# A shared pool of PSUM pairs, a planner with a clock and SiLU as one function, in an RWKV-7 scan followed by a SwiGLU layer

## The chip, the cores and the metric

The kernel runs on one core of a Trainium2 chip. The metric is device time in microseconds of one execution; three executions of the kernel before took 1606.69 to 1614.95 us, median 1608.68 us. Five engines work side by side: PE (TensorE, matrix products, with weight loads PEld that can overlap them), DVE (VectorE), ACT (ScalarE), POOL (GpSimd) and SP (SyncE), which here issues every DMA. Each engine runs its own instructions in the order in which the program gives them, and waits on semaphores for the others.

## The reference

Two blocks in a row. First a recurrent attention over S = 768 steps for 4 x 8 heads of width D = 40; then a feed-forward layer over the 3072 tokens of width 320 (8 heads x 40).

```python
for t in range(S):
    y[:, :, t] = einsum('bhd,bhde->bhe', r_t, state)
    Sa = einsum('bhde,bhe->bhd', state, a_t)
    state = state * w_t[:, :, None, :] - einsum('bhd,bhe->bhde', Sa, b_t) + einsum('bhd,bhe->bhde', v_t, k_t)
x = y as (3072, 320)
xn = x / sqrt(mean(x * x) + 1e-6) * rms_g
g = xn @ w_gate;  val = xn @ w_val            # 320 x 1536 each
out = (g * sigmoid(g) * val) @ w_out          # 1536 x 320
```

The scan's inputs are float32, the feed-forward weights float64: the kernel narrows them to float32 by bit operations. All matrix products are in float32.

## The kernel before, in words

**The work.** The 768 steps are cut into 24 chunks of C = 32 steps, all 32 heads at once. Per chunk there are four routines, all of which only *register* their operations with a planner:

- `front(c)` (line 337) loads w, a, k, b, v (ten DMAs), turns two of the tiles on PE, and walks five levels (1, 2, 4, 8, 16). Each level makes a group of 64 small matmul instructions `gr` (line 222, profile name `psB<-A,K`), a masked copy into `LT` (`where`, line 195), scalings of K and A on DVE, ACT and POOL, and from the second level on a turned copy `KN` (a transpose of eight 128x128 blocks, `turned`, line 317, profile name `psB<-ident,K`, and an ACT copy). It ends with DMAs that bring the chunk's 32 x 32 matrices through DRAM (`sB`) into the layout `M`.
- `inverse(c)` (line 401) inverts these unit triangular matrices on DVE: 31 steps of a product into `tmp` and a subtraction into `Yi` (lines 411 and 412, recorded under the helper's line 183), then DMAs back through `sY` into `LT`. There is one `M` tile.
- `main(c)` (line 421) carries the state over the chunk: products X, U, `up` and the new state `ST`; then the outputs `y` by one product with the state and five by levels, the root mean square, and the scaled, turned rows `xg`. Most of its PE pieces are groups of 64 small matmuls (`psC<-...`), five are transposes.
- `feed(g)` (line 535) does the feed-forward layer for two chunks once both `xg` parts are there: 12 slices f of the hidden width. Each slice loads `wf` (480 KB) and runs a group H (`psH<-xg,wf`, 12 matmul instructions of 256 columns), and each a group O (`psO<-wf,hT`, 4 instructions of 320 columns) which is added up in `psO` over all 12. Two slices share one H tile: after both H groups ACT takes the sigmoid of the gate half (512 columns, line 207), DVE multiplies gate and sigmoid, DVE multiplies by the value half into `hT`, and the two O groups follow.

`narrow` (line 568) is called 24 times ahead of the loop. Each call loads a part of the weights, and works it into float32 with seven DVE operations of 480 columns (lines 188, 192, 183: `sg<-wf`, `hT<-wf`, twice `sg<-sg`, `sg<-wf,sg`, `hT<-wf,hT`, `hT<-hT,sg`) and one on ACT (`hT<-hT`), and stores it to DRAM (`sW`). It borrows the buffers `wf`, `sg` (2) and `hT` (2) of `feed`.

**PSUM.** PSUM holds four tiles of [128, 2, 512] float32 (a pair of banks each), one per role (line 308): B for everything in `front`, C for everything in `main`, H and O for `feed`. The next user of a role's pair waits until the last one has been read out.

**The order.** `Plan` (line 26) is a list scheduler that runs while the program is built. `Plan.add` (line 46) registers a *piece* (one instruction, or one PE group) with an engine, a due time, an estimated time and its tiles; it derives which earlier pieces it needs from overlapping regions. `Plan.issue` (line 70) lets a simulated time run per engine: an engine that is free takes, of the pieces whose needs are met by then, the one due first. The order in which the pieces were taken is the program's order. Due times are laid out by a period of T = 46 per chunk: `front(c)` from (c - 2) T, `inverse(c)` from (c - 1) T + 4, `main(c)` from c T, the 12 slices of `feed(g)` from 2 (g + 1) T over two periods, `narrow` number f from -46 + 8 f. A PE group is taken as 0.6 to 2.2 us whatever the engine's clock; a DMA holds SP for 0.06 us and lands 2.2 us plus its bytes later, whatever else is moving.

Before all of this the program clears the tiles that are only partly written later: `Turns` (line 263) with its flag set clears them whole, on DVE and POOL by turns.

Of the kernel before, what the change touches and what calls it, by code (L numbers as in the profile page):

```python
# [7 lines left out]
FP32 = mybir.dt.float32  # L8
# [13 lines left out]
T = 46.0  # L22
EPS = 1e-6


class Plan:
# [3 lines left out]
    LATENCY = 0.1  # L30

    def __init__(self):
        self.pieces = []
        self.needs = []
        self.seen = {}

    @staticmethod
    def box(ap):
        dims = list(ap.ap)
        if ap.tensor.space == DRAM:  # L40
# [5 lines left out]
    def add(self, engine, due, time, issue, outs, ins, more=0.0):  # L46
        me = len(self.pieces)
        needs = set()
        mine = {}
        for aps, write in ((ins, False), (outs, True)):  # L50
            for ap in aps:
                key = ap.tensor.name, write
                a = self.box(ap)
                if key in mine:
                    b = mine[key]
                    a = min(a[0], b[0]), max(a[1], b[1]), min(a[2], b[2]), max(a[3], b[3])
                mine[key] = a
# [9 lines left out]
        self.pieces.append((engine, due, time, more, issue))  # L67
        self.needs.append(needs)

    def issue(self):  # L70
        n = len(self.pieces)
        users = [[] for _ in range(n)]
        missing = [len(d) for d in self.needs]
        for i, d in enumerate(self.needs):
            for j in d:
                users[j].append(i)
        ready = [0.0] * n
        free, waiting, order = {}, {}, []
        for i in range(n):
            free.setdefault(self.pieces[i][0], 0.0)  # L80
            waiting.setdefault(self.pieces[i][0], [])
            if not missing[i]:
                waiting[self.pieces[i][0]].append(i)
        for _ in range(n):
            best = None
            for e, w in waiting.items():
                if w:
                    t = max(free[e], min(ready[i] for i in w))
                    if best is None or t < best[0]:
                        best = t, e  # L90
            t, e = best
            i = min((i for i in waiting[e] if ready[i] <= t), key=lambda i: (self.pieces[i][1], i))
            waiting[e].remove(i)
            _, _, time, more, _ = self.pieces[i]
            free[e] = t + time
            order.append((t, i))
            for j in users[i]:
                ready[j] = max(ready[j], t + time + more + self.LATENCY)
                missing[j] -= 1
                if not missing[j]:  # L100
                    waiting[self.pieces[j][0]].append(j)
        for _, i in sorted(order):
            self.pieces[i][4]()
        self.order = sorted(order)
# [3 lines left out]
def kernel(  # L108
# [65 lines left out]
    plan = Plan()  # L174
# [6 lines left out]

    def tt(due, o, a, b, op):
        plan.add("DVE", due, 0.145 + 0.00104 * size(o), lambda: nc.vector.tensor_tensor(o, a, b, op), [o], [a, b])  # L183

    def ts(due, o, a, s1, s2, op1, op2=None):
        ins = [a] + [x for x in (s1, s2) if isinstance(x, bass.AP)]
        args = (op1,) if op2 is None else (op1, op2)
        plan.add("DVE", due, 0.145 + 0.00104 * size(o), lambda: nc.vector.tensor_scalar(o, a, s1, s2, *args), [o], ins)

    def stt(due, o, a, s, b, op1, op2):  # L190
        plan.add("DVE", due, 0.145 + 0.00104 * size(o),
                 lambda: nc.vector.scalar_tensor_tensor(o, a, s, b, op1, op2), [o], [a, b])

    def where(due, o, m, a):
        plan.add("DVE", due, 0.16 + 0.00104 * size(o), lambda: nc.vector.copy_predicated(o, m, a), [o], [m, a, o])  # L195

    def copy(due, o, a):
        plan.add("ACT", due, 0.16 + 0.00083 * size(o), lambda: nc.scalar.copy(o, a), [o], [a])  # L198

    def scale(due, o, a, by):  # L200
        ins = [a, by] if isinstance(by, bass.AP) else [a]
        plan.add("ACT", due, 0.16 + 0.00083 * size(o), lambda: nc.scalar.mul(o, a, by), [o], ins)  # L202

    def act(due, o, a, f, acc=None, **kw):
        if acc is not None:
            kw["accum_out"] = acc
        plan.add("ACT", due, 0.16 + 0.00083 * size(o), lambda: nc.scalar.activation(o, a, f, **kw),  # L207
                 [o] + ([acc] if acc is not None else []), [a])

    def ptt(due, o, a, b, op):  # L210
        plan.add("POOL", due, 0.2 + 0.0021 * size(o), lambda: nc.gpsimd.tensor_tensor(o, a, b, op), [o], [a, b])  # L211

    def pcopy(due, o, a):
        plan.add("POOL", due, 0.15 + 0.0014 * size(o), lambda: nc.gpsimd.tensor_copy(o, a), [o], [a])

    def dma(due, o, i, by="SP"):
        q, t = {"SP": (nc.sync, 0.06), "POOL": (nc.gpsimd, 1.0)}[by]
        n = size(i) * list(i.ap)[0][1]
        plan.add(by, due, t, lambda: q.dma_start(out=o, in_=i), [o], [i], 2.2 + n * 4 / 200e3)  # L219

    def mm(o, lhsT, rhs, start=True, stop=True):
        return o, lhsT, rhs, lambda: nc.tensor.matmul(o, lhsT, rhs, start=start, stop=stop, skip_group_check=True)  # L222

    def flip(o, i, ident):
        return o, i, ident, lambda: nc.tensor.transpose(o, i, ident)  # L225

    def pe(due, time, steps):
# [411 lines left out]
```

## Time and profile before

| | before |
|---|---|
| time, median of 3 (lowest, highest) | 1608.68 us (1606.69, 1614.95) |
| the profiled execution: time, span | 1605.55 us, 1603.8 us |
| PE busy, share of the span | 1384.5 us, 86% |
| DVE, ACT, POOL busy | 854.5, 441.6, 206.1 us |
| mean granted clock of PE | 0.902 |
| first and last H group start | 238.0, 1592.1 us |

How to read it: the page's first part has the busy time per engine; the second cuts the span in 40 slices of 40.1 us with the busy tenths of each engine and the granted PE clock. PE has two clock levels, 1.2 and 2.4 GHz; a granted clock of 0.50 is the lower one. The view of windows gives the busy time, the number of instructions (x) and the granted clock of any stretch. The timeline lists instructions in order of time, like ones merged, with the idle time before them and what ended it in brackets. The view of groups gives, per kind of instruction, the total busy time, the mean of one in ns, and the idle time of the engine just before them. Every helper records its own line, so groups are told apart by their tiles.

### The profile page before, as it was taken

What the parts mean: (1) busy time and instruction counts of PE and PEld (TensorE: products, weight loads), DVE (VectorE), ACT (ScalarE), POOL (GpSimd) and SP (SyncE); (2) the same over time, 40 slices, a digit from 0 to 9 for tenths busy, and PEclk for the clock granted to TensorE, in tenths of its full rate; (3) what the DMA queues carried; (4) which work ended last, traced back from release to release, by engine and by line L of the source; (5) the groups of instructions that cost most, each with busy time, mean ns of one, the idle gap of its engine ahead of it and who ended that gap; (6) DMA issues with size and microseconds to landing.
All of it is one profiled execution on the core that took longest, in us unless ns stands there. A gap on an engine that the chain in (4) does not pass through costs nothing.

```text
span 1603.8 us, 65497 instructions
## 1 busy us (share of the span) xinstructions
PE 1384.5 (86%) x29632; PEld 1110.6 (69%) x29632; DVE 854.5 (53%) x2767; ACT 441.6 (28%) x805; POOL 206.1 (13%) x360
## 2 busy tenths in 40 slices
PE   4556679889989999889989989989989989989766
PEld 3556677677777777667777777767778777767644
DVE  7777764545555565545555555644645554643211
ACT  2232323133323223232332323323323323212100
POOL 4110210111111110111110110110110110100000
PEclk9999979798999799798999789989989779799878
DMA  7453523243343343343343343333343344232211
GB/s 151 140 153 100 147 46 88 75 99 80 88 103 80 84 104 83 80 104 75 88 104 79 89 99 86 82 99 79 89 100 85 83 99 95 60 87 83 84 50 45
DMA packets 300246, 146.19 MB, mean 91 GB/s; under 512 B 263104, under 2 KB 276928, under 8 KB 299968
## 3 DMA queue, kind: packets, MB, share of 16 engines
q1 hardware_dynamic: 299968, 142.01, 36.4%
q8 instruction: 232, 3.80, 1.0%
q14 instruction: 46, 0.38, 0.1%
HBM read 125.83 MB, written 16.12 MB: 89 GB/s over the span
## 4 chain that ended last, share of the span: by engine, by line
PE 71%; DVE 8%; issue 6%; DMA 6%; ACT 5%; SPq 3%; POOL 1%; DVEq 0%; POOLq 0%; ACTq 0%
PE psH L222 22%; PE psC L222 17%; PE psO L222 11%; PE psB L225 9%; PE psB L222 7%; PE psC L225 5%; SPq L219 3%; DMA kbn<-in_b_dram 2%; DMA M<-sB 2%; ACT Xs L202 1%; DVE hT L183 1%; DVE y L183 1%; DMA sB<-LT 1%; ACT K L198 1%; DVE tmp L183 1%
## 5 line engine op out<-in xcount | busy, mean ns | idle before, releaser
L222 PE MATMUL psH<-xg,wf 128*128 128x256 f32 (+1 forms) x1728 | 411.8, 430 | 2.0 <-DVE xg L183 1.4
L222 PEld LDWEIGHTS psH<-xg,wf 128*128 128x128 f32 (+1 forms) x1728 | 278.3, 205 | 95.8 <-issue 55.4
L183 DVE TENSOR_TENSOR tmp<-Yi,M 128x60 f32<-128x60 f32 (+24 forms) x744 | 179.5, 241 | 98.8 <-DMA M<-sB 83.7
L222 PE MATMUL psO<-wf,hT 128*128 128x320 f32 x576 | 209.2, 490 | 19.1 <-DVE hT L183 18.3
L222 PEld LDWEIGHTS psB<-A,K 40*64 40x64 f32 x7680 | 154.9, 163 | 62.0 <-issue 30.0
L222 PE MATMUL psB<-A,K 40*64 40x16 f32 x7680 | 165.7, 226 | 32.2 <-ACT K L198 18.4
L183 DVE TENSOR_TENSOR Yi<-Yi,tmp 128x60 f32<-128x60 f32 (+24 forms) x744 | 177.3, 238 | 15.6
L225 PE MATMUL psB<-ident,K 128*128 128x128 f32 x960 | 152.7, 310 | 29.0 <-DVE LT L195 23.9
L198 ACT COPY KN<-psB 128x640 f32<-128x640 f32 x120 | 83.1, 693 | 293.9 <-PE psB L225 274.6
L183 DVE TENSOR_TENSOR sg<-psH,sg 128x512 f32<-128x512 f32 x72 | 49.7, 690 | 207.3 <-ACT sg L207 207.3
L225 PEld LDWEIGHTS psB<-ident,K 128*128 128x128 f32 x960 | 125.2, 160 | 39.7 <-DVE LT L195 24.9
L222 PEld LDWEIGHTS psO<-wf,hT 128*128 128x128 f32 x576 | 106.9, 206 | 55.1 <-DVE hT L183 21.8
L211 POOL TENSOR_TENSOR A<-A,T 128x256 f32<-128x256 f32 x96 | 73.0, 760 | 525.5 <-ACT T L198 176.9
L222 PEld LDWEIGHTS psC<-As,KN 64*64 64x64 f32 x6144 | 110.0, 147 | 37.2 <-issue 32.5
L222 PE MATMUL psC<-As,KN 64*64 64x16 f32 x6144 | 118.7, 216 | 17.8 <-issue 10.0
L183 DVE TENSOR_TENSOR K<-K,T 128x512 f32<-128x512 f32 (+1 forms) x192 | 100.5, 523 | 57.6 <-PE psB L225 38.2
L207 ACT ACTIVATE sg<-psH 128x512 f32<-128x512 f32 x72 | 43.1, 598 | 289.6 <-PE psH L222 289.5
L195 DVE COPY_PREDICATED LT<-msk,psB 128x256 f32<-128x256 uint32 x120 | 66.1, 551 | 88.4 <-PE psB L222 87.1
L198 ACT COPY K<-K 128x256 f32<-128x256 f32 x240 | 87.4, 415 | 32.8 <-DVE K L183 28.6
L183 DVE TENSOR_TENSOR y<-y,psC 128x256 f32<-128x256 f32 (+1 forms) x192 | 58.8, 318 | 67.9 <-PE psC L222 66.3
L183 DVE TENSOR_TENSOR As<-psC,msk 128x256 f32<-128x256 f32 x120 | 41.9, 414 | 45.9 <-PE psC L222 45.9
L225 PE MATMUL psB<-ident,kbn 128*128 128x128 f32 x192 | 37.1, 357 | 27.2 <-DMA kbn<-in_b_dram 21.3
(96 smaller groups left out, 1384.1 us busy)
## 6 DMA issues: line engine op xcount, KB each, us to landing
wf<-sW SPq DMA_DIRECT2D x144, 480.0 KB, 3.5
M<-sB SPq DMA_DIRECT2D x96, 128.0 KB, 3.5
sW<-hT SPq DMA_DIRECT2D x24, 240.0 KB, 3.4
wan<-in_w_dram SPq DMA_DIRECT2D x48, 80.0 KB, 3.1
wan<-in_a_dram SPq DMA_DIRECT2D x48, 80.0 KB, 3.1
kbn<-in_k_dram SPq DMA_DIRECT2D x48, 80.0 KB, 3.1
kbn<-in_b_dram SPq DMA_DIRECT2D x48, 80.0 KB, 3.2
VU<-in_v_dram SPq DMA_DIRECT2D x48, 80.0 KB, 2.7
```

The lines of the kernel that those rows point to most:

```text
L183: plan.add("DVE", due, 0.145 + 0.00104 * size(o), lambda: nc.vector.tensor_tensor(o, a, b, op), [o], [a, b])
L195: plan.add("DVE", due, 0.16 + 0.00104 * size(o), lambda: nc.vector.copy_predicated(o, m, a), [o], [m, a, o])
L198: plan.add("ACT", due, 0.16 + 0.00083 * size(o), lambda: nc.scalar.copy(o, a), [o], [a])
L202: plan.add("ACT", due, 0.16 + 0.00083 * size(o), lambda: nc.scalar.mul(o, a, by), [o], ins)
L207: plan.add("ACT", due, 0.16 + 0.00083 * size(o), lambda: nc.scalar.activation(o, a, f, **kw), [o] + ([acc] if acc is not None else []), [a])
L211: plan.add("POOL", due, 0.2 + 0.0021 * size(o), lambda: nc.gpsimd.tensor_tensor(o, a, b, op), [o], [a, b])
L219: plan.add(by, due, t, lambda: q.dma_start(out=o, in_=i), [o], [i], 2.2 + n * 4 / 200e3)
L222: return o, lhsT, rhs, lambda: nc.tensor.matmul(o, lhsT, rhs, start=start, stop=stop, skip_group_check=True)
L225: return o, i, ident, lambda: nc.tensor.transpose(o, i, ident)
```

## The change

- `Plan` is given three PSUM pairs and a list of eight stand-in tensors. A stage that needs PSUM takes `plan.room()`; which pair it gets is chosen in `issue` when its first piece is taken: a piece that opens a room is not ready until a pair is free, and the pair is free again when the room's last piece is done. H, B and C stages all draw on these three; O keeps a pair of its own.
- `issue` has a clock of its own for PE, at 1.0 or 0.5, that follows the `columns` of the pieces it has put into the last stretch, by the constants in the class; times of PE pieces are divided by it. Pieces with `columns` of 500 or more are H (2560), O (1280), the transposes of eight blocks (1024); all others count 0, but `xg`'s transposes (384). When the clock is low, or few columns have been streamed lately, PE takes only such pieces if any can go. Pieces marked `paced=True` (H and O) are held back until the due time of the pieces of `main` (`paced=None`) comes near.
- The estimates change: 0.08 us more per PE group, a DMA holds SP for 0.45 us and takes its turn in one lane of 180 GB/s.
- `feed` works slice by slice: H, then SiLU as one ACT function on 256 columns, one DVE product of 256 columns, and O due one slice later. Its due times are 10 later (`LAG`).
- `narrow` is due from 60 + 6 f. Of its DVE operations two become ACT functions (Relu with scale and bias) and the last a POOL product.
- Tiles of which only the padding must be zero are cleared there alone. In `main` the two groups of X, and the first groups of y, change places.

```diff
 class Plan:
-    LATENCY = 0.1
+    LATENCY = 0.15
+    WINDOW, ENOUGH, KEEP = 3.41, 1600, 1300
+    LOOK, LOW = 1.0, 1400
+    AHEAD, FAR = 4.0, 30.0
...
+    def room(self):
+        name = list(self.stand_ins)[len(self.rooms) % len(self.stand_ins)]
+        self.now[name] = len(self.rooms)
+        self.rooms.append([0, None, None])
+        return self.stand_ins[name]
...
+        def put(i):
+            p = P_[i]
+            (held if p.paced and p.due > pace + self.FAR else waiting[p.engine]).append(i)
+        def at_least(i):
+            p = P_[i]
+            return max(p.ready, min(pairs)) if p.room is not None and self.rooms[p.room][1] is None else p.ready
...
+            t, e = min((max(free[e], min(at_least(i) for i in w)), e) for e, w in waiting.items() if w)
+            can = [i for i in waiting[e] if at_least(i) <= t]
+            if e == "PE":
+                at = int(t / self.WINDOW)
+                while len(clock) <= at:
+                    c = columns.get(len(clock) - 1, 0)
+                    clock.append(1.0 if c >= (self.ENOUGH if clock[-1] < 1 else self.KEEP) else 0.5)
...
+                many = [i for i in can if P_[i].columns >= 500]
+                if many and (clock[at] < 1 or had < self.LOW):
+                    can = many
+                else:
+                    can = [i for i in can if not P_[i].paced or P_[i].due <= pace + self.AHEAD] or can
+            i = min(can, key=lambda i: (P_[i].due, i))
...
+                if room[1] is None:
+                    room[1] = min(range(len(pairs)), key=lambda q: pairs[q])
+                    pairs[room[1]] = float("inf")
+                room[0] -= 1
+                if not room[0]:
+                    pairs[room[1]] = end + self.LATENCY
...
-    plan = Plan()
+    plan = Plan([psum.tile([P, 2, 512], FP32, name=f"ps{i}") for i in range(3)],
+                [dram.tile([P, 2, 512], FP32, name=f"room{i}") for i in range(8)])
...
-    def dma(due, o, i, by="SP"):
-        q, t = {"SP": (nc.sync, 0.06), "POOL": (nc.gpsimd, 1.0)}[by]
-        plan.add(by, due, t, lambda: q.dma_start(out=o, in_=i), [o], [i], 2.2 + n * 4 / 200e3)
+    def dma(due, o, i):
+        plan.add("SP", due, 0.45, lambda at: nc.sync.dma_start(out=o, in_=i), [o], [i], lane=max(0.5, n * 4 / 180e3))
...
-                (nc.vector, nc.gpsimd)[i % 2].memset(t, 0.0)
+                (nc.vector, nc.gpsimd)[i % 2].memset(zero(t), 0.0)
...
-    ps_ = {t: Turns(n, [P, 2, 512], "ps" + t, pool=psum) for t, n in (("C", 1), ("B", 1), ("H", 1), ("O", 1))}
+    po_ = psum.tile([P, 2, 512], FP32, name="po")
...
-            act(d + 4, sg, h[:, 0], AF.Sigmoid)
-            tt(d + 4, sg, h[:, 0], sg, MUL)
-            tt(d + 5, hT, h[:, 1], sg, MUL)
+            act(d + 3, sg, h[:, 0], AF.Silu)
+            tt(d + 4, hT, h[:, 1], sg, MUL)
...
+        act(d, exf, ex, AF.Relu, scale=-1.0, bias=c1151)
+        act(d, ex, exf, AF.Relu, scale=-8388608.0, bias=c255)
-        ts(d, ex, ex, -896.0, 0.0, ALU.add, ALU.max)
-        ts(d, ex, ex, 255.0, 8388608.0, ALU.min, ALU.mult)
-        tt(d, m, m, ex.bitcast(FP32), MUL)
+        ptt(d, m, m, exf, MUL)
...
-        d = -T + 8 * f
+        d = N0 + NF * f
```

Here `N0, NF = 60.0, 6.0`, and `T = 46.0` as before.

## Rows read from the trace of the kernel before

**Rows 1.** The page: busy times, and the granted clock in 40 slices.

```profile
PE 1384.5 (86%) x29632; PEld 1110.6 (69%) x29632; DVE 854.5 (53%) x2767; ACT 441.6 (28%) x805; POOL 206.1 (13%) x360
...
PEclk9999979798999799798999789989989779799878
```

**Rows 2.** Windows: stretch, length, busy time (count) per engine, PEclk, DMA share, GB/s.

```profile
0.00:204.40 204.40, 121.27 (x2386) 107.91 (x2387) 153.15 (x443) 56.88 (x106) 42.05 (x73) 1.00 0.55 136
204.40:238.00 33.60, 25.25 (x791) 22.51 (x789) 18.67 (x76) 9.58 (x20) 4.77 (x8) 0.70 0.30 55
238.00:1472.00 1234.00, 1140.12 (x25115) 909.02 (x25112) 658.28 (x2196) 361.75 (x655) 157.70 (x275) 0.89 0.37 88
1472.00:1534.80 62.80, 48.43 (x1161) 38.07 (x1160) 16.08 (x42) 9.11 (x17) 1.57 (x4) 0.84 0.22 71
1534.80:1603.80 69.00, 49.40 (x192) 33.09 (x192) 8.30 (x12) 4.27 (x7) 0.00 (x0) 0.90 0.18 55
```

**Rows 3.** Timeline of PE, start and length in us: light groups, early and after 204 us.

```profile
21.73 1.91 PE L222 MATMUL psB<-A,K 40*64 40x16 f32 x64 [5.04 <-ACT K L198]
...
46.71 1.97 PE L225 MATMUL psB<-ident,K 128*128 128x128 f32 x8 [0.78 <-ACT KN L198]
...
205.65 1.12 PE L222 MATMUL psB<-A,K 40*64 40x16 f32 x64
```

**Rows 4.** Timeline of PE from 279 us: before and after a heavy group.

```profile
279.08 1.91 PE L222 MATMUL psC<-As,KN 64*64 64x16 f32 x64
...
286.95 3.90 PE L222 MATMUL psH<-xg,wf 128*128 128x256 f32 x12
...
296.23 2.63 PE L222 MATMUL psH<-xg,wf 128*128 128x256 f32 x12
```

**Rows 5.** Groups of PE between 238 and 1472 us: busy, mean ns, idle before.

```profile
L225 PE MATMUL psB<-ident,kbn 128*128 128x128 f32 x152 | 27.2, 338 | 21.6 <-DMA kbn<-in_b_dram 20.4 <-ACT A L198 0.6 <-DMA wan<-in_w_dram 0.3
...
L225 PE MATMUL psC<-ident,x 128*128 128x128 f32 x60 | 15.6, 371 | 17.6 <-ACT x L202 17.0 <-POOL x L214 0.7
```

**Rows 6.** Windows of the first two inversions, all operations.

```profile
53.80:90.40 36.60, 17.95 (x356) 15.74 (x354) 34.88 (x124) 9.30 (x19) 4.91 (x9) 1.00 0.46 135
109.70:173.50 63.80, 38.87 (x920) 35.31 (x920) 47.98 (x156) 17.09 (x32) 6.55 (x9) 1.00 0.45 124
```

**Rows 7.** The same windows, only what uses Yi.

```profile
53.80:90.40 36.60, 14.04 (x62) 0.00 (x0) 1.00 0.46 135
109.70:173.50 63.80, 15.30 (x62) 0.00 (x0) 1.00 0.45 124
```

**Rows 8.** The same windows, only what uses sg.

```profile
53.80:90.40 36.60, 16.00 (x32) 0.00 (x0) 1.00 0.46 135
109.70:173.50 63.80, 20.63 (x43) 0.00 (x0) 1.00 0.45 124
```

**Rows 9.** Groups by shape: what SiLU and narrow replace, and their nearest rows.

```profile
L183 DVE TENSOR_TENSOR sg<-psH,sg 128x512 f32<-128x512 f32 x72 | 49.7, 690 | 207.3 <-ACT sg L207 207.3
...
L183 DVE TENSOR_TENSOR As<-psC,msk 128x256 f32<-128x256 f32 x120 | 41.9, 414 | 45.9 <-PE psC L222 45.9
...
L207 ACT ACTIVATE sg<-psH 128x512 f32<-128x512 f32 x72 | 43.1, 598 | 289.6 <-PE psH L222 289.5
...
L198 ACT COPY y<-psC 128x256 f32<-128x256 f32 x24 | 8.9, 372 | 45.6 <-PE psC L222 45.6
...
L207 ACT ACTIVATE hT<-hT 128x480 f32<-128x480 int32 x24 | 14.5, 605 | 32.1 <-DVE hT L188 32.1
...
L211 POOL TENSOR_TENSOR Sdec<-ST,T 128x640 f32<-128x640 f32 x24 | 30.8, 1284 | 170.6 <-DVE ST L183 151.7 <-DVE Yi L183 18.8
...
L207 ACT ACT_TABLE_LOAD x1 | 1.3, 1283 | 0.0
```

**Rows 10.** Timeline of PE in the last feed, with its waits.

```profile
1544.14 1.34 PE L222 MATMUL psO<-wf,hT 128*128 128x320 f32 x4 [2.15 <-DVE hT L183]
...
1594.66 2.42 PE L222 MATMUL psO<-wf,hT 128*128 128x320 f32 x8 [2.15 <-DVE hT L183]
```

More of the change, by code (lines that the diff above doesn't have):

```diff
@@ L44, in box, with add @@
         return p, p + dims[0][1], f, f + sum(s * (n - 1) for s, n in dims[1:]) + 1
-    def add(self, engine, due, time, issue, outs, ins, more=0.0):
+    def add(self, engine, due, time, issue, outs, ins, **kw):
         me = len(self.pieces)
+        piece = Piece(engine, due, time, issue, **kw)
         needs = set()
@@ new lines, in add @@
+        piece.missing = len(needs)
+        for i in needs:
+            self.pieces[i].users.append(me)
+        if piece.room is not None:
+            room = self.rooms[piece.room]
+            room[2] = first = me if room[2] is None else room[2]
+            for i in needs:
+                if i < first and first not in self.pieces[i].users:
+                    self.pieces[i].users.append(first)
+                    self.pieces[first].missing += 1
+            room[0] += 1
+        self.pieces.append(piece)
@@ L224, in flip, with pe, issue @@
     def flip(o, i, ident):
-        return o, i, ident, lambda: nc.tensor.transpose(o, i, ident)
-    def pe(due, time, steps):
-        def issue():
+        return o, i, ident, lambda at: nc.tensor.transpose(at(o), i, ident)
+    def pe(due, time, steps, columns=0, paced=False, more=[]):
+        def issue(at):
             for s in steps:
-                s[3]()
-        plan.add("PE", due, time, issue, [s[0] for s in steps], [x for s in steps for x in s[1:3]])
+                s[3](at)
+        plan.add("PE", due, time + 0.08, issue, [s[0] for s in steps] + more, [x for s in steps for x in s[1:3]],
+                 columns=columns, paced=paced)
@@ L441, in main @@
                  U[rows(i, 1), :, 0:N * D].rearrange("p o (n d) -> p o n d", n=N))
-        up = ps_["C"].next()
-        pe(d + 8, 0.95, [mm(up[half(o), i, col(n)], kn(z, 32, i, n, o), VU[half(i), n, o, 0:D]) for n, i, o in each])
+        up = plan.room()
+        pe(d + 8, 0.95, [mm(up[half(o), i, col(n)], kn(z, 32, i, n, o), VU[half(i), n, o, 0:D]) for n, i, o in each], paced=None)
         if c + 1 < NCH:
@@ L479, in level @@
         def level(due, ps, j):
-            pe(due, 0.95, [mm(ps[half(o), i, n], kn(z, LEVELS[j], i, n, o), As[half(i), j, o * N + n]) for n, i, o in each])
+            pe(due, 0.95, [mm(ps[half(o), i, n], kn(z, LEVELS[j], i, n, o), As[half(i), j, o * N + n]) for n, i, o in each], paced=None)
         def down(due, j, ps):
@@ L514, in main @@
             down(d + 30 + q, j, yl[:, :, q])
-        xn = ps_["C"].next()
+        xn = plan.room()
         pe(d + 35, 0.6, [mm(xn[half(q), o, m * D:(m + 1) * D],
```

258 lines of the change are left out of this document (143 added, 115 removed).

## The prediction

> **What bounds the kernel now.** I read the page's busy times first: PE works 86% of the span, DVE 53%, so PE is the engine to account for, and the row of granted clocks shows that it is seldom at full speed for long [rows 1]. Then the windows by stage [rows 2]. Between 238 us, when the first H group starts, and 1472 us PE is busy 1140 of 1234 us at a granted clock of 0.89: 94 us idle, and, as the two levels are 1.0 and 0.5, (1 - 0.89) x 2 = 22% of the stretch, 271 us, at the lower one. If PE is as busy there as elsewhere (92%), 250 us of its work ran at half speed and about 125 us of them are lost. So the stretch holds about 1140 - 125 = 1015 us of work at full clock. Before 238 us stand 238 us in which PE is busy 147 us with the scan alone. The stretch to 204 us reads 1.00, but only because the record of the clock starts there: a group of 64 small matmuls takes 1.91 us at 21 us and 1.12 us at 205 us, and the transposes at 46 us, 1.97 us, are at the lower level too [rows 3]. After 1472 us come 132 us of draining. Between 276 and 290 us is a typical loss: light groups at 1.91 us, an H group that takes 3.90 us and pulls the clock up, and the next H at 2.63 us [rows 4].
>
> So the span is 1015 us of dense work, 125 us of half clock, 94 us of idle PE, 238 us of start and 132 us of end.
>
> **The change part by part**, on the profiled execution's own 1605.55 us (span 1603.8 us and 1.75 us around it; the median of the runs is 3.1 us above it).
>
> *A, the start: -45 us.* The state can't move to the next chunk before that chunk's inversion is done. The first takes 36.6 us and the second 63.8 us on DVE [rows 6], though their own 62 operations need only 14.0 and 15.3 us [rows 7]; operations on `sg`, all of them narrowing at this time, take 16.0 and 20.6 us of DVE in the same windows [rows 8]. `narrow` was due from -46, among the inversions; it is now due from 60, behind both, and three of its seven operations leave DVE. Counting only what is counted in rows 8, 16 + 20.6 = 37 us go. With one pair per role the front pass also waits at each step for a copy out of PSUM, 0.78 us in the row at 46 us [rows 3], and about ten such waits stand in the first pass: 8 us more. Bounds: 71 us, if both inversions fall to their own times, and 0, if the narrowing, which must end before the first H as it shares its buffers, now ends no earlier: its chain gets longer by one ACT step (605 ns in its row, twice, in place of two DVE steps) and a POOL step (under the 1284 ns of the 640-element product) [rows 9]. I take 45, nearest to what is counted. POOL and ACT have room, 13% and 28% busy [rows 1]. If that room failed, the queue behind a waiting `narrow` step on DVE is the inversion itself, and PE waits for that.
>
> *B, the clock from 238 to 1472 us: -80 us.* The new order puts H, O or transposes into any stretch that runs light. There are enough of them: a chunk has 6 H groups (2.63 us [rows 4]), 6 O groups (1.34 us [rows 10]) and about 10 transposes (about 1 us, half of the 1.97 us at the lower level [rows 3]): some 34 of the roughly 50 us that a chunk takes at full clock (1015 us for some 20 chunks in the stretch). Bounds: 0 and 125. The row at 286 us, where one H group brings the clock back, speaks for the far end; the order is fixed while the program is built, and PE's true times will slip against the planner's, so I leave about a third: -80.
> A row here differs from a rule. The clock first rises at 204 us, in a stretch of 64-matmul groups and transposes, 34 us before the first H: transposes at least don't prevent it [rows 2, 3]. The Trainium skill (TensorE: Matmul & The Clock Gate, Part 4, on PE-mode transpose) says that full rate does not engage for transposes, as they don't count as busy in the same way. By that rule only H and O would hold the clock, B would shrink towards 0 and the sum would be 1518 us in place of 1438 us; the first rival below has the same time from rows.
>
> *C, idle PE in the same stretch: -24 us.* Of the 94 us, 21.6 us stand before the transposes of `kbn`, waiting for its DMA, and 17.6 us before those of x, waiting for a chain over ACT and POOL [rows 5]. The new planner counts 0.45 us of SP per DMA in place of 0.06 and so will issue `kbn` earlier, and with three shared pairs PE has another stage's group to fill the second. Bounds: +94 (twice as much, from waits for pairs) and -94. I take the sum of the two rows, 39 us, less some 15 us for new waits. What is late next: PE itself.
>
> *D, the end: -22 us.* The last feed has PE to itself: in the 69 us from 1534.8 us it is busy 49.4 us [rows 2]. Two H groups fill the one H pair, then PE waits 2.15 us for sigmoid and two products, six times in all [rows 10]: 13 us, of which the last wait stays, shorter (one ACT function and one product). Of these 13 us I take 11. A granted clock of 0.90 means 20% of the window at the lower level, so some 10 us of the 49.4 us, of which 5 go with a PE that doesn't pause. From 1472 to 1534.8 us 14 us are idle; I take 6 of them, for feed slices held ready. Bounds 0 and 34 (all idle of both windows).
>
> *SiLU itself: 0.* DVE loses 72 products of 690 ns and turns 72 others of 512 columns into 144 of 256, 414 ns by the nearest row: about -39 us. ACT gets 144 functions, 372 ns by the copy of 256 columns from PSUM, for 72 of 598 ns: +11 us. Both lie beside PE; only in D is the chain on the path. If SiLU shared no activation table with the other functions, each of the 24 squares would cost two loads of 1283 ns [rows 9], 62 us of ACT, hidden by its idle time; I take 0, since sigmoid, copy and square need one load together in this trace after the first. If that cover went, the wait would stand before x.
>
> *Clearing padding only* shortens what DVE does ahead of the first chunk by a few us, inside A's bounds. The exchange of the two X groups, of y's groups and the later due times: 0; the instructions on PE stay the same.
>
> Sum: 45 + 80 + 24 + 22 = 171 us; 1605.6 - 171 = 1434.6, and 3.1 us for the median: **1438 us**.
>
> **The rivals.**
> *The heavy pieces don't hold the clock.* A, C and D come, B doesn't: 1438 + 80 = 1518 us. For it: the order of before had all these groups too and spent 22% at the lower level [rows 2]. Against it: one H group is followed by the full rate [rows 4].
> *Slower: the pool of three pairs starves PE.* A pair is now taken about 12 times per chunk by `front`, 11 by `main` and 3 by `feed`, 26 x 24 = 624 times. Each taker waits for a read-out that the planner has guessed, and PE's order is fixed: a late copy holds everything behind it, of all roles. If half of the takes meet the wait of 0.78 us [rows 3], that is 243 us: 1438 + 243 = 1681 us. It decides from (171 + 8) / 624 = 0.29 us per take on. Against it: a take holds a pair for about 3 us, 26 x 3 = 78 us per chunk of 50 us, on three pairs, which is half of what they offer.
> *The planner's clock is out of step.* The order comes out with the idle time and the half clock of before, and the longer narrowing chain eats A: 1605 us, nothing that can be told.
>
> **How the numbers follow.** The forecast case gets 0.70: its own range, from B and C at their better ends with A at 71 (1438 - 26 - 45 - 30 = about 1335), to A at 0 (1483 us). The clock rival gets 0.18 (1480 to 1560), out of step 0.04, starving 0.08. A measurement of this kernel tells about 0.5%, 8 us, from no change. Faster: 0.70 + 0.18 = 0.88; same 0.04; slower 0.08. The range from 1335 to 1545 us holds nearly all of the first case and four fifths of the second, a little over 0.8.
>
> **What would show it.** A: the first H before 200 us, both inversions under 45 us. B: a granted clock over 0.95 from the first H to 1470 us, and few H groups at 4 us or more. C: idle PE under 75 us in as long a stretch of work, without a large wait of PE on a copy or on DVE. D: under 58 us from the last `xg` to the end, H and O without gaps. SiLU: `sg` products gone, ACT at 144 functions near 372 ns, no table loads in the loop. Wrong it would be if PE waited for read-outs before many first groups of a pair (starving), or if the clock stayed near 0.89 while H, O and transposes are spread evenly (the clock rival).

## The result, and the profile after

The changed kernel takes **1429.48 us**, median of 4 runs (1421.51 to 1436.31); the kernel before takes 1607.68 us in the same comparison (4 runs, 1600.68 to 1614.95). The ratio is **0.889, with a 95% interval from 0.883 to 0.895**: 178 us faster. The profiled execution of after took 1430.57 us, span 1428.8 us; below it is set against the one of before with its span of 1603.8 us. In the comparison of E1 to E4 one execution of E1 and one of the kernel before were over 1.5% slower than the fastest of their kernel, and they are left out of the medians and ratios.

From the page of after: busy times, the granted clock in 40 slices of 35.7 us, and the engines' shares of the chain that ended last. They answer to [rows 1].

```profile
PE 1289.4 (90%) x29632; PEld 1048.9 (73%) x29632; DVE 851.9 (60%) x2695; ACT 486.5 (34%) x925; POOL 233.1 (16%) x386
...
PEclk8755666999997989999999989999999999999999
...
PE 51%; DVE 34%; issue 5%; SPq 4%; DMA 3%; ACT 3%; POOL 0%; DVEq 0%; POOLq 0%; ACTq 0%
```

PE runs the same 29632 instructions in 1289.4 in place of 1384.5 us. For equal instructions a shorter busy time means a higher clock, so some 95 us of the gain are clock. Idle PE (span less busy) falls from 219.3 to 139.4 us, 80 us. Together these are the whole 175 us of the two spans. The third row warns of what is next: a third of the chain stands on DVE now, where before it was 8%.

The windows of after by stage, in the columns of [rows 2]: to the first H; the dense stretch, to the end of the last front work; the drain, to the last `xg`; the last feed.

```profile
0.00:241.70 241.70, 171.59 (x4263) 156.83 (x4264) 192.98 (x538) 113.07 (x204) 83.25 (x119) 0.65 0.53 129
241.70:1315.00 1073.30, 1011.35 (x23768) 814.02 (x23768) 632.39 (x2081) 355.11 (x682) 148.28 (x264) 0.96 0.41 98
1315.00:1377.70 62.70, 62.63 (x1413) 48.25 (x1411) 20.88 (x66) 12.70 (x27) 1.57 (x4) 1.00 0.28 84
1377.70:1428.80 51.10, 43.87 (x192) 29.78 (x192) 5.62 (x13) 5.59 (x14) 0.00 (x0) 0.98 0.32 98
```

PE has two clock levels, and a stretch is taken to lose half of the busy time that it spends at the lower one (an estimate: a group of 64 takes 1.91 us there for 1.12). The table counts that record by record of the granted clock. Both traces read 1.00 up to their first record (204.4 us in before, 13.7 us in after), though the durations of PE's work show the lower level; this time is counted as low. By the rows' rounded clocks alone, (1 - clock) x busy, the dense stretch comes out alike: 125 and 40 us.

| stage | idle PE, before and after | lost to the clock | the rest: work at full clock |
|---|---|---|---|
| start, to the first H | 91.5, 70.1 | 67, 65 | 79, 107 |
| the dense stretch | 93.9, 62.0 | 120, 43 | 1020, 969 |
| drain and last feed | 34.0, 7.3 | 10, 0 | 88, 106 |
| sum | 219.4, 139.4 | 197, 108 | 1187, 1182 |

The work must come out equal in sum; its 5 us of difference show how exact the table is.

**Who PE waits for now.** Groups of PE in the dense stretch of after; columns as in [rows 5], whose two rows are the last two here.

```profile
L310 PE MATMUL ps<-ident,VU 128*128 128x128 f32 x160 | 23.2, 292 | 12.9 <-DVE tmp L270 8.7 <-DVE Yi L270 4.1
...
L310 PE MATMUL ps<-ident,ST 128*128 128x128 f32 x152 | 22.7, 297 | 26.3 <-DVE tmp L270 22.6 <-DVE Yi L270 2.1 <-DVE LT L270 1.6
...
L310 PE MATMUL ps<-ident,kbn 128*128 128x128 f32 x144 | 18.8, 273 | 0.0
...
L310 PE MATMUL ps<-ident,x 128*128 128x128 f32 x60 | 10.5, 284 | 0.0
```

The waits for `kbn`'s DMA (21.6 us) and for x (17.6 us) are gone, and new ones stand before the transposes of the state, of VU and of r. The profile puts them down to `tmp` and `Yi`, steps of the inversion. But no transpose of `main` reads either, so the name can't be taken as it stands. The largest of these waits, in the timeline of PE and then of DVE (start us, length us):

```profile
608.14 1.12 PE L307 MATMUL ps<-A,K 40*64 40x16 f32 x64
609.10 1.12 PE L307 MATMUL ps<-VU,KN 64*64 64x40 f32 x64
614.58 1.76 PE L310 MATMUL ps<-ident,VU 128*128 128x128 f32 x7 [4.36 <-DVE tmp L270]
```

```profile
613.33 0.23 DVE L270 TENSOR_TENSOR Yi<-Yi,tmp 128x72 f32<-128x72 f32 x1
613.48 0.42 DVE L270 TENSOR_TENSOR hT<-ps,sg 128x256 f32<-128x256 f32 x1
613.81 0.71 DVE L270 COPY_PREDICATED LT<-msk,ps 128x256 f32<-128x256 uint32 x1
614.32 0.25 DVE L270 TENSOR_TENSOR tmp<-Yi,M 128x68 f32<-128x68 f32 x1
```

`tmp` ends at 614.57 us, 0.01 us before PE starts, and so it is named. The masked copy `LT<-msk,ps` ends at 614.52, 0.06 us before: it reads the group `ps<-A,K` of 608.14 us out of its PSUM pair, and stood for over 4 us in DVE's queue, mostly behind inversion steps. Gone through one by one, the dense stretch has 33 waits of PE of over 0.3 us, 48 us in all, that end 0.054 to 0.056 us after such a copy, and 5 (8 us) that end as long after `hT<-ps,sg`. 4 of the 5 stand before another group of a shared pair, the fifth before an O. The program's own instructions name the buffer: in all 33 and in these 4 the waiting group writes the very pair that this operation has just read. So PE waits for a **pair to be read out**, and the read-out stands in DVE's queue among the inversion: from the end of the group that it reads to its own start, the 33 copies lose 95 us together, 79 us of them with inversion steps at work.

### The profile page after: what moved, and what is told of

Its sections match the earlier page's. It is cut to its first block, busy times and chain, and to the rows that moved or that the text cites. A ratio compares the mean times of both kernels' runs of the same rounds, so it can differ in the third digit from the quotient of the medians.

```text
span 1428.8 us, 65724 instructions
## 1 busy us (share of the span) xinstructions
PE 1289.4 (90%) x29632; PEld 1048.9 (73%) x29632; DVE 851.9 (60%) x2695; ACT 486.5 (34%) x925; POOL 233.1 (16%) x386
## 4 chain that ended last, share of the span: by engine, by line
PE 51%; DVE 34%; issue 5%; SPq 4%; DMA 3%; ACT 3%; POOL 0%; DVEq 0%; POOLq 0%; ACTq 0%
PE ps L307 35%; DVE Yi L270 11%; DVE tmp L270 11%; PE ps L310 8%; PE po L307 7%; SPq L304 3%; DVE K L270 3%; DVE T L270 3%; DVE LT L270 2%; DVE hT L270 1%; DMA sB<-LT 1%; DMA M<-sB 1%; DVE ST L270 1%; ACT sg L287 1%; DVE As L270 1%
## 5 line engine op out<-in xcount | busy, mean ns | idle before, releaser
L307 PE MATMUL ps<-xg,wf 128*128 128x256 f32 (+1 forms) x1728 | 389.2, 413 | 0.7 <-DVE xg L270 0.7
L307 PEld LDWEIGHTS ps<-xg,wf 128*128 128x128 f32 (+1 forms) x1728 | 262.1, 195 | 85.1 <-issue 52.2
L307 PE MATMUL po<-wf,hT 128*128 128x320 f32 x576 | 190.8, 458 | 0.4 <-DVE hT L270 0.4
L310 PE MATMUL ps<-ident,K 128*128 128x128 f32 x960 | 145.4, 307 | 26.3 <-DVE K L270 20.7
L307 PEld LDWEIGHTS ps<-A,K 40*64 40x64 f32 x7680 | 132.6, 142 | 40.9 <-issue 26.5
L307 PE MATMUL ps<-A,K 40*64 40x16 f32 x7680 | 143.5, 212 | 12.1 <-DVE hT L270 4.2
L310 PEld LDWEIGHTS ps<-ident,K 128*128 128x128 f32 x960 | 123.6, 158 | 37.0 <-issue 26.4
L307 PEld LDWEIGHTS po<-wf,hT 128*128 128x128 f32 x576 | 101.7, 195 | 31.8 <-issue 4.7
L307 PEld LDWEIGHTS ps<-As,KN 64*64 64x64 f32 x6144 | 108.1, 145 | 21.3 <-issue 13.4
L307 PE MATMUL ps<-As,KN 64*64 64x16 f32 x6144 | 116.3, 214 | 4.3 <-DVE As L270 3.0
```

What stands on the lines that cost most here:

```text
L307: return o, lhsT, rhs, lambda at: nc.tensor.matmul(at(o), lhsT, rhs, start=start, stop=stop, skip_group_check=True)
L310: return o, i, ident, lambda at: nc.tensor.transpose(at(o), i, ident)
```

## The experiments

All are edits of the changed kernel. Beside each span stand PE's busy time, and idle as span less busy, from the page of each run; the clock is that of the dense stretch, from the first H to the end of the last front work. The runs come from five comparisons, in which the kernel before had medians from 1600 to 1608 us; so differences between medians are good to some 8 us, and the ratios say more.

| run | median us | ratio to before, 95% | span | PE busy | idle | clock |
|---|---|---|---|---|---|---|
| after | 1429.48 | 0.889 (0.883 to 0.895) | 1428.8 | 1289.4 | 139 | 0.96 |
| E1 no clock | 1512.20 | 0.947 (0.933 to 0.960) | 1510.4 | 1358.7 | 152 | 0.92 |
| E2 roles | 1497.98 | 0.937 (0.930 to 0.945) | 1495.9 | 1317.6 | 178 | 0.95 |
| E3 sigmoid | 1459.11 | 0.913 (0.904 to 0.921) | 1463.4 | 1321.4 | 142 | 0.93 |
| E4 narrow at 0 | 1420.64 | 0.891 (0.883 to 0.900) | 1417.4 | 1281.0 | 136 | 0.95 |
| E5 same order | 1447.13 | 0.905 (0.900 to 0.910) | 1454.0 | 1301.1 | 153 | 0.95 |
| E6 old estimates | 1479.03 | 0.923 (0.918 to 0.928) | 1478.2 | 1300.8 | 177 | 0.94 |
| E7 lag 0 | 1416.62 | 0.884 (0.879 to 0.889) | 1416.5 | 1283.5 | 133 | 0.97 |
| E8 calibrated | 1441.01 | 0.901 (0.896 to 0.907) | 1434.5 | 1283.6 | 151 | 0.95 |
| E9 half inversion | 1297.18 | 0.810 (0.806 to 0.813) | 1293.7 | 1237.0 | 57 | 1.00 |
| E10 lag 0, narrow 0 | 1409.82 | 0.879 (0.876 to 0.882) | 1407.8 | 1269.8 | 138 | 0.97 |
| E11 lag 0, DVE +0.03 | **1363.42** | 0.852 (0.847 to 0.856) | 1361.9 | 1248.5 | 113 | 0.99 |
| E12 DVE model | 1420.51 | 0.887 (0.883 to 0.891) | 1416.3 | 1266.0 | 150 | 0.97 |

**E1: the planner's clock taken away.** It always counts full speed, and prefers nothing.

```diff
-        clock, columns, recent, lane, order = [0.5], {}, [], 0.0, []
+        clock, columns, recent, lane, order = [1.0], {}, [], 0.0, []
-                    clock.append(1.0 if c >= (self.ENOUGH if clock[-1] < 1 else self.KEEP) else 0.5)
+                    clock.append(1.0)
-                if many and (clock[at] < 1 or had < self.LOW):
+                if False:
```

> The changed kernel without the planner's clock: it takes PE to run at full rate always and no longer prefers H, O and transposes when few columns were streamed; the pool, the other estimates, SiLU and the narrowing stay. Theory 1 (the preference holds the clock): the dense stretch from the first H to 1315 us falls back from a granted clock of 0.96 to about 0.89, which gives back the 77 us of half clock: about 1505 us. Rival (the pool alone gives the order, the clock is a by-product): clock of 0.94 or more in that stretch, 1429 to 1445 us.

1512 us, 83 us more than after. The dense stretch of E1, in the columns of [rows 2]:

```profile
284.30:1382.60 1098.30, 1025.72 (x22714) 827.23 (x22713) 593.63 (x1975) 341.77 (x662) 146.06 (x254) 0.92 0.38 93
```

Of the 82 us between the spans PE's busy time takes 69, so it is the clock. In the dense stretch it falls only to 0.92, between the two forecasts: 88 us are lost there, counted as in the table above, against 43 in after and 120 in before. But the first H moves to 284 us, and 86 us are lost ahead of it, against 65 in after. Over the whole execution PE's busy time is 1384.5 us in before, 1358.7 us in E1 and 1289.4 us in after: 69 of the 95 us hang on the planner's clock and its preference for heavy groups, which E1 takes away together. What brings the other 26 us is not shown.

**E2: the pool taken away.** Three pairs as before, each bound to a role again; the rest of the planner stays.

```diff
-    def room(self):
+    def room(self, role):
-        self.rooms.append([0, None, None])
+        self.rooms.append([0, None, None, role])
-            return max(p.ready, min(pairs)) if ...
+            return max(p.ready, pairs[self.rooms[p.room][3]]) if ...
-                    room[1] = min(range(len(pairs)), key=lambda q: pairs[q])
+                    room[1] = room[3]
```

> The changed kernel with its clock, but the three pairs given one to each role again (front, main, feed), as before. Theory 1 (the preference holds the clock, the pool only saves idle time): granted clock still about 0.95 from the first H on, idle PE in that stretch up by the 32 us that the change took away: about 1460 us. Rival (the pool is what gives the planner a choice): clock back at 0.90 and idle up as well, 1530 us or more.

1498 us: the pool is worth some 69 us. The windows of drain and last feed of E2, in the columns of [rows 2], and PE's timeline at the start of the last feed:

```profile
1348.20:1434.90 86.70, 72.25 (x1408) 54.88 (x1406) 17.53 (x50) 12.85 (x26) 2.83 (x5) 0.83 0.24 71
1434.90:1495.90 61.00, 46.13 (x192) 30.92 (x192) 5.65 (x13) 5.29 (x13) 0.00 (x0) 0.95 0.21 62
```

```profile
1440.83 1.34 PE L307 MATMUL po<-wf,hT 128*128 128x320 f32 x4 [1.00 <-DVE hT L270]
1442.02 2.52 PE L307 MATMUL ps<-xg,wf 128*128 128x256 f32 x12
1445.48 2.63 PE L307 MATMUL ps<-xg,wf 128*128 128x256 f32 x12 [0.94 <-DVE hT L270]
```

The last feed has one pair again and waits 0.9 to 1.0 us at H and at O; the drain has idle time and half clock again. This is neither of the two times that had been expected. Idle time and loss of E2, counted stage by stage as in the table above, are over those of after by 14 us in the start, 20 us in the dense stretch (idle 71 us for 62, clock 0.95 for 0.96) and 36 us in drain and last feed. So the pool works most at the end.

**E3 and E5: SiLU as two steps again.** E3 takes a sigmoid and one more product of 256 columns on DVE, known to the planner. E5 keeps the order of after to the instruction: the product goes right ahead of the other, and the planner doesn't know of it.

```diff
-            act(d + 3, sg, h[:, 0], AF.Silu)
+            act(d + 3, sg, h[:, 0], AF.Sigmoid)
+            tt(d + 3, sg, h[:, 0], sg, MUL)
```

> The changed kernel with sigmoid on ACT and a product on DVE in place of SiLU, still slice by slice. Theory 1: 144 more products of some 0.42 us on DVE, 60 us, lie beside PE; no change, 1421 to 1437 us. Rival (the chain from H to O and DVE's queue are near the path, as the chain of waits is now 34% DVE): 1445 us or more, with PE waiting longer behind DVE.

> Sigmoid with an additional DVE product of 256 columns per slice, but the planner is told nothing of the product, so that every engine keeps exactly the order of the changed kernel. It parts two readings of the 30 us that sigmoid cost when the planner knew of it. Reading 1 (the longer chain and DVE's queue cost it): about 1455 to 1465 us again, the dense stretch at a granted clock near 0.93. Reading 2 (another order, that happens to hold the clock worse): 1425 to 1437 us, at 0.96.

E3 takes 1459 us, 30 more than after, as its rival had said; of the 35 us between the spans 32 are PE's busy time. E5 takes 1447 us, 18 more, which lies between its two readings. So about 18 us are the price of 144 more products in DVE's queue and the longer chain; the other 12, which are hardly clear of the noise, would come with another order. In the profiled execution of E5, its slowest, the waits that end 0.05 us after `LT` grow from 48 to 58 us and those after `hT` from 8 to 14: the product, in a queue that is idle for 37% of the span, makes read-outs late.

**E4 and E8: the narrowing earlier.** E4 lets it be due from 0 in place of 60. E8 does the same and also gives the planner H and transposes with the times that the trace of after shows.

```diff
-N0, NF = 60.0, 6.0
+N0, NF = 0.0, 6.0
```

> The changed kernel with the narrowing due from 0 in place of 60. Theory 1 (the first H, at 241.7 us, waits for the narrowing, whose last store is issued at 241.8 us, not for the scan, whose second xg is there at 193 us): first H at about 200 us, and the 40 us of earlier feed work fill light time: 1405 to 1415 us. Rival (earlier narrowing again pushes the inversions apart): second xg 20 us later or more, no gain, 1425 to 1445 us.

> Narrowing due from 0, and PE estimates moved to what the chip shows: 2.50 us for H (2.28 before), 0.95 us for eight transposes (1.03 before). If slip between the planner's clock and the chip's is what leaves 43 us of half clock in the dense stretch: half of that goes, about 1400 us. Rival (the slip comes from DVE and ACT, not from PE's own times): 1415 to 1430 us.

In E4 the last narrowed part is stored at 189 us and the first H starts at 194.6 us; in after they stand at 241.8 and 241.7 us. The rows of stores `sW` on SP's queue (first and last start), of E4 and then, for 225 to 250 us, of after:

```profile
L304 SPq DMA_DIRECT2D sW<-hT x24: 319/379/1409, 40.5 to 189.0; - x24
```

```profile
L304 SPq DMA_DIRECT2D sW<-hT x3: 338/433/444, 230.9 to 241.8; - x3
```

So the narrowing is the gate of the first H: shown. But 47 us of earlier H are worth 9 us by the medians (1420.6 against 1429.5; 15 to 24 were expected) and nothing by the ratios (0.891 against 0.889). To its first H, E4 has done some 80 us of PE's work at full clock, against 107 in after: in after PE used the time ahead of the gate for other work. E8 misses both of its forecasts and is 20 us slower than E4: PE's own times, told better, didn't help, and nothing shows that the slip comes from them.

**E6: the old estimates** for latency (0.1 us), DMAs (0.06 us of SP, no lane) and PE groups (0.08 us less) in the new planner.

```diff
-    LATENCY = 0.15
+    LATENCY = 0.1
...
```

> The changed kernel with the estimates of the kernel before: 0.08 us less per PE group, a DMA at 0.06 us of SP and landing 2.2 us plus its bytes later, 0.10 us between engines. Theory (estimates near the chip's own times keep PE's fixed order and the planner's clock in step): PE waits for DMA of kbn again, some 20 us in the dense stretch, and the clock there falls towards 0.92: 1455 to 1480 us. Rival (estimates hardly matter, pool and clock do it): 1429 to 1437 us.

1479 us, in the range of the theory: the three estimates together are worth 50 us, mostly idle PE (177 us). But not by an earlier `kbn`, for which PE doesn't wait here either. The waits of PE in the dense stretch of E6 (total us, times, longest):

```profile
PE po L306 <- DVE hT L269: 49.1, 25, 4.1
```

In after that wait is 0.4 us. With these shorter estimates the planner puts O where `hT` isn't ready yet. Which of the three does it was not tried.

**E9: how much is DVE's queue?** The order of after to the instruction, without the 744 subtractions `Yi`: half of the inversion's steps, a part of the computation, is left out.

```diff
-            tt(d + i, Y[:, 0:n, i + 1:], Y[:, 0:n, i + 1:], tmp, SUB)
+            o = Y[:, 0:n, i + 1:]
+            plan.add("DVE", d + i, 0.145 + 0.00104 * size(o), lambda at: None, [o], [o, tmp])
```

> The changed kernel in exactly its own order, but the 31 subtractions of each inversion are left out of the program (part of the computation is missing, and the matrices stay the unit ones); the planner still counts them. DVE loses 744 operations, some 180 us, all beside PE. Theory (what PE waits for in the dense stretch is DVE's queue, in which the inversion stands ahead of the state and of read-outs): idle PE there falls from 62 us to under 30 us, and the clock, which slips with it, gains some 10 us: 1375 to 1395 us. Rival (the waits are set by the pairs and by the order itself): 1415 us or more.

1297 us, 132 less than after and below what either theory gave. Its dense stretch, and two groups of PE in it:

```profile
208.90:1176.60 967.70, 960.16 (x23746) 783.22 (x23746) 467.25 (x1465) 350.00 (x679) 153.15 (x263) 1.00 0.45 108
```

```profile
L310 PE MATMUL ps<-ident,ST 128*128 128x128 f32 x152 | 20.0, 274 | 0.0
L310 PE MATMUL ps<-ident,VU 128*128 128x128 f32 x152 | 19.9, 274 | 0.0
```

PE is idle for 7.5 us in 968, the clock is at 1.00, and the waits before the transposes are 0.0, with the same planned order and the same pairs. With DVE's 744 operations the waits go, and the half clock that was left goes with them. PE is at its floor here, so the remaining 43 + 62 us of the dense stretch, and 33 us at the start, where the first H now comes at 208.9 us, hang on DVE, which is busy for 60% of the span in after. E9 also ends each inversion sooner, and doesn't part this from a shorter queue; that the queue does it rests on the single waits shown further up.

**E7, E10, E11, E12: other orders by the same planner.** E7 was meant as a control (`LAG = 0.0`), E10 joins it with E4. E11 is E7 with 0.03 us more for each DVE operation. E12 is E10 with a closer model: each operation holds DVE for 0.08 us less, but who depends on it, or takes its pair, waits 0.13 us more.

```diff
-LAG = 10.0
+LAG = 0.0
-        plan.add("DVE", due, time + 0.00104 * size(o), ...
+        plan.add("DVE", due, time + 0.03 + 0.00104 * size(o), ...
```

> A control: the feed due 10 us earlier (LAG 0 in place of 10), nothing else; another order of the same pieces by the same planner. If orders of the same planner differ little on the chip: 1422 to 1440 us. If a chance order is worth tens of us, as reading 2 of the run with the same order says: off by 20 us or more in either direction, by the half clock of the dense stretch.

> The two settings that came out ahead, together: feed due 10 us earlier (LAG 0) and narrowing from 0. If the 13 us and the 9 us add up: about 1407 us. If each was a chance of its order: anywhere from 1405 to 1440 us.

> LAG 0, and every DVE operation counted 0.03 us longer by the planner, nearer to the 0.25 us that a step of the inversion takes from one to the next where nothing stands between. If the slip of the planner against the chip comes from DVE: PE waits less behind DVE, 1395 to 1410 us. Rival (orders of this planner scatter by some 15 us, whatever the estimate): 1410 to 1435 us.

> LAG 0, narrowing from 0, and DVE told apart in the planner as the trace has it: an operation keeps the engine for about 0.07 us plus its columns, but its result is there only 0.13 us later, for the next DVE operation that needs it too (a step of the inversion follows the other after 0.19 us plus its columns, an operation that needs nothing of it after 0.08 us plus them). If the slip of DVE's estimate is the cause of what is lost in the dense stretch: at least as good as the run with 0.03 us more per operation, 1340 to 1365 us. Rival (the flat 0.03 us helped by its slack, or as a chance of the order; a tight estimate has none): 1380 to 1420 us.

E7 is 13 us faster than after by the medians and 8 by the ratios, whose intervals overlap: a lag alone can do that much, and a difference of that size between two orders proves no cause. E10, at 1410 us, lies where both of its readings had put it. **E11 takes 1363.42 us (1361.38 to 1369.37), 0.852 of before and 66 us below the change itself** (60 by the ratios), the best complete version here, and below both ranges that had been given. Its dense stretch, and the largest of PE's waits in it:

```profile
242.50:1239.00 996.50, 970.41 (x23776) 789.08 (x23775) 615.00 (x2061) 346.59 (x680) 149.84 (x260) 0.99 0.44 105
```

```profile
PE po L307 <- DVE hT L270: 6.8, 11, 1.1
PE ps L310 <- DVE Yi L270: 5.6, 6, 1.0
```

In E7 the first of these rows is 27.5 us. E12 is a miss: 1421 us where 1340 to 1365 had been expected. So a planner that knows how steps follow each other on the chip isn't enough for what E11 gains. Either it is the slack itself, or that 0.03 us x 2695 operations = 81 us come near what DVE loses beside POOL (last section), which E12 left out; and a part may be chance, as in E7. No run tells these apart.

## Why the prediction was right, and where it wasn't

The time, 1438 against 1429 us, and the range held. Not all the steps did, and that the sum came so near is partly luck. Idle time and lost clock of the profiled executions fall by 24 us in A for the 45 of the sum, by 77 in B for 80, by 32 in C for 24 and by 37 in D for 22: 170 us for 171, as A's shortfall meets what C and D bring beyond theirs. The lower end of the range is also not what its sentence says: it takes C 30 us further, not the 70 us to C's better end.

- **B, the clock: right in size, and in most of its mechanism.** -80 us predicted; 120 to 43 us of loss, -77. The granted clock from the first H on is 0.96, as the sign for it said, and H groups of 4 us or more fall from 17 to 7 in the dense stretch. E1 shows that the planner's clock with its preference brings 69 of the 95 us of PE's busy time; in the forecast all of it hung on that. The clock rival's 1518 us is near what E1 measures without them, 1512 us.
- **C, idle PE in the dense stretch: right in size (-32 for -24), wrong in its list.** The two waits went, as said, and idle PE is 62 us, under 75. But the sign "without a large wait of PE on a copy or on DVE" failed: 56 us of waits for read-outs by DVE took their place. The failed sentence is "What is late next: PE itself." Late next is DVE's queue. The prediction left DVE, 53% busy, out of the account; what counts is that a read-out of a pair stands in order behind inversion steps, which run later than planned.
- **The starving rival had the right mechanism at the wrong price.** It let PE wait for a late read-out, with everything behind it held. This happens, but for 56 us over 624 takes in 0.09 us each, not the 0.39 us put there, and below the 0.29 us from which it decides. E2 shows the other side: without the pool it is 69 us slower.
- **A, the start: the scan came out as said, the gate did not.** The inversions did fall, further than forecast, to 16.7 and 17.8 us. The windows of the first two in after, to be set beside [rows 6]:

```profile
57.30:74.00 16.70, 1.60 (x67) 1.33 (x64) 14.60 (x64) 1.34 (x3) 2.10 (x3) 0.52 0.22 63
79.70:97.50 17.80, 8.61 (x272) 8.08 (x271) 15.77 (x69) 3.43 (x7) 1.40 (x3) 0.60 0.22 51
```

  The second `xg` is there at 192.7 in place of 235.9 us, 43 us sooner. But the first H didn't come before 200 us: it starts at 241.7 us, 3.7 us later than before. In before the narrowing's last store starts at 191.2 us and the first H follows the second `xg` after 2 us; in after the last store starts at 241.8 us. So the change itself made the narrowing end 50 us later, and made it the gate. E4 shows it: with the narrowing early, the first H again follows the second `xg` (192.8 us) after 2 us. The lower bound had named it ("the narrowing, which must end before the first H as it shares its buffers, now ends no earlier"), but the 45 us were counted without it. E4 shows one thing more: a first H 47 us sooner isn't worth 47 us, as PE has other work to do ahead of it. What there was to gain came in another way: 28 us more of PE's work is done ahead of the gate, and idle time and loss fall by 21 + 3 us.
- **D, the end: right, and better than said.** From the last `xg` 51.1 us (under 58 predicted, 69.0 before); idle PE over both windows falls by 27 us for the 17 counted, lost clock by 10 for 5. The groups of PE in the last feed of after, for [rows 10]:

```profile
L307 PE MATMUL ps<-xg,wf 128*128 128x256 f32 (+1 forms) x144 | 30.5, 400 | 0.7 <-DVE xg L270 0.7
L307 PE MATMUL po<-wf,hT 128*128 128x320 f32 x48 | 14.8, 448 | 0.0
```

  The six waits of 2.15 us are gone: three pairs let the next H go while SiLU runs. In E2, with one pair for it again, waits of 0.9 to 1.0 us stand there: the pool takes these away.
- **SiLU itself: 0 was wrong.** The durations were right (ACT 385 ns for 372, DVE 422 for 414, no table load after the two of 1283 ns at the start). What failed is "Both lie beside PE". By E5 and E3 it is worth 18 to 30 us; the waits of E5 say how: each product less on DVE lets a read-out come sooner.
- **The narrowing's new steps** cost more than the rows they were taken from. Groups of after before 241.7 us:

```profile
L287 ACT ACTIVATE sg<-sg,c 128x480 f32<-128x480 int32 (+1 forms) x48 | 33.3, 697 | 20.3 <-DVE sg L270 19.7
...
L297 POOL TENSOR_TENSOR hT<-hT,sg 128x480 f32<-128x480 f32 x24 | 31.7, 1322 | 111.2 <-DVE hT L270 94.1 <-PE ps L310 10.3 <-DVE sg L270 6.8
...
L270 DVE SCALAR_TENSOR_TENSOR sg<-wf,sg 128x480 int32<-128x480 int32 x24 | 19.4, 807 | 10.9 <-ACT sg L287 10.9
```

  ACT takes 697 ns for the 605 counted, and the POOL product of 480 columns 1322 ns, over the 1284 ns that had been taken as its upper bound from one of 640. Both lengthen the chain of a narrowed part. What moved the gate, though, is the later due time: in E4, with the same steps, the last store starts at 189 us, about where it was in before.
- **Clock out of step**, the rival at 1605 us, was not seen, but the slip that it rests on was: E6 shows 50 us that hang on the estimates, through DVE's results and not, as C had it, through `kbn`.

## What to carry to other kernels

In a program with one fixed order for each engine, an engine that is 60% busy can still set the time, when it is the one that reads PSUM out: look at what stands ahead of the read-outs in its queue, not at its share. When the profile names as releaser an instruction that the waiting one doesn't need, look at what ended just before it; a constant distance (here 0.055 us) over many waits finds the true one, and the buffer names in the program confirm it. A start with a gate is costed by the gate, and a change can move the gate (here from the scan to the narrowing). A planner's estimates are part of the kernel: 0.03 us more per DVE operation and a lag of 0 gave another 66 us here, while a model that looks closer (E12) gave nothing.

## What the runs showed of the hardware that was not expected

**DVE is stretched beside POOL.** The timelines of after, DVE first, then POOL:

```profile
943.89 0.22 DVE L270 TENSOR_TENSOR Yi<-Yi,tmp 128x72 f32<-128x72 f32 x1
944.15 1.25 DVE L270 TENSOR_TENSOR tmp<-Yi,M 128x68 f32<-128x68 f32 x1
945.44 0.70 DVE L270 TENSOR_TENSOR Yi<-Yi,tmp 128x68 f32<-128x68 f32 x1
```

```profile
944.06 1.26 POOL L297 TENSOR_TENSOR Sdec<-ST,T 128x640 f32<-128x640 f32 x1 [2.97 <-DVE ST L270]
945.41 0.64 POOL L297 TENSOR_TENSOR A<-A,T 128x256 f32<-128x256 f32 x1
```

A step of 0.22 us takes 1.25 us, until the POOL product beside it ends, and the next one 0.70 us in the same way. The view of single tiles in after (shortest, median and longest in ns) shows which operations this meets:

```profile
L270 DVE TENSOR_TENSOR tmp<-Yi,M x744: 165/218/1267, 57.3 to 1318.0; 128x60 f32<-128x60 f32 x18, 128x54 f32<-128x54 f32 x12, 128x66 f32<-128x66 f32 x12, 128x28 f32<-128x28 f32 x12
```

```profile
L270 DVE TENSOR_TENSOR hT<-ps,sg x144: 412/424/426, 246.7 to 1420.3; 128x256 f32<-128x256 f32 x144
```

`tmp`, with both inputs in SBUF, reaches 1267 ns; `hT`, with one input in PSUM, never leaves 412 to 426 ns. Adding, over all DVE operations that overlap one of POOL, what each took beyond the median of its operation and shape (where over 0.1 us) gives 96 us of DVE's 852 in after, in 208 operations, 58 us of it in the inversion; in before it is 82 us, so the change didn't bring it. The Trainium skill (SBUF — State Buffer, Who interferes with whom) says that a VectorE instruction with two SBUF inputs contends with a GpSimd instruction that reads SBUF, and that the port pair that they share is an exclusive lock. These rows agree: the step of 1.25 us ends 0.08 us after the POOL product beside it. No planner's estimate here knows of it, so it is one cause of DVE's slip behind the plan that can be seen. How much of the time hangs on it was not tried: that needs a kernel with POOL's products elsewhere.

**Transposes alone raised the clock.** PE's first work in after, in its timeline:

```profile
9.61 1.94 PE L310 MATMUL ps<-ident,wan 128*128 128x128 f32 x8 [9.61 <-DVE msk L333]
11.35 1.91 PE L310 MATMUL ps<-ident,kbn 128*128 128x128 f32 x8
14.37 1.12 PE L307 MATMUL ps<-A,K 40*64 40x16 f32 x64 [1.10 <-ACT K L291]
15.57 1.06 PE L310 MATMUL ps<-ident,K 128*128 128x128 f32 x8
```

After 16 transposes and nothing else, a group of 64 takes 1.12 us, its time at full rate in [rows 3], and eight transposes take 1.06 in place of 1.94 us. The Trainium skill (TensorE: Matmul & The Clock Gate, Part 4, on PE-mode transpose) says that full rate doesn't engage for transposes. Here the rows differ from it, and the measurement decides: the prediction was right not to follow the rule, which by its working would have led to 1518 us.

**A step that needs the one before it starts later.** At 941.71 us in after `tmp` of 76 columns starts, and the independent `hT` follows 0.16 us later; a `tmp` of 60 columns at 941.20 us is followed by its own `Yi` after 0.26 us. E12 built on that difference and gained nothing.
